# An attention kernel followed by two mixtures of experts: the first batch's pooled probabilities are turned ahead of its value sums, two of four token sums move to GpSimd, and the list of due times is set anew

## The chip, the cores and the metric

The kernel runs on one core of one Trainium2 chip. The metric is the device time of one execution in microseconds (us). The engines are named as in the profile: PE is TensorE's matrix multiply, PEld its weight load, DVE is VectorE, ACT is ScalarE, POOL is GpSimd, SP issues most of the transfers.

## The reference

Three stages follow each other; a sketch of what is computed:

```python
# q, k, v: [4 batches, 8 heads, 576 tokens, 64]
pooled = softmax(mean4(q) @ mean4(k).T / 8) @ mean4(v)   # 144 pooled tokens, each repeated 4 times
local  = softmax(where(|i - j| < 4, q @ k.T / 8, -1e9)) @ v
x = (repeat4(pooled) + local)           # -> [2304 tokens, 512]
h = x @ w_in                            # 512 -> 2048
x = (h * cos(h)) @ w_out                # 2048 -> 512
xn = x / sqrt(mean(x * x) + 1e-6) * rms_g
y = (silu(xn @ w_gate) * (xn @ w_val)) @ w_out2   # 512 -> 1536 -> 512
```

## The kernel before

**Tiles.** The 2304 tokens are nine tiles of 256. Attention makes them, batch by batch: `pooled` (L553) does one pair of heads of the pooled part, `block` one block of 116 tokens of the local part, `join` (L934) adds the two and `to_x` splits the sum into a high and a low part (L919 on ACT, L921 on POOL). The first product of experts runs in units of 512 columns, over a tile or a pair of tiles: `h` (L1200), then `kk` (L1218, ACT), `t` (L1220, DVE), the sine (L1223, ACT), the product with h (L1225, DVE), the high part `gh` (L1234, ACT), the low part `gl` (L1236, on DVE or POOL), and `y` (L1266), which multiplies `gh` and `gl` by the second weights. Tiles 0 to 4 go through alone (512 columns are then two weight slices of a 256-wide tile), tiles 5, 6 and 7, 8 in pairs. Each precise product is three fast ones (high by high, high by low, low by high). The gated product behind it (L1689, L1942) fills the second half of the time.

**The opening.** Before the first tile can start, SP loads the first heads of q and k, PE turns them (`qtr`, L680, in `turn`, L671), their tokens are summed in fours (L687, DVE), and `pooled` takes batch 0's four head pairs through scores (`sps`, L573), softmax (L578 to L594), a transpose of the probabilities (`tra`, L609), the value product (`avp`, L633) and a copy into `od`. The values' own pooled sums come from `pv` (L433). The local blocks run between: scores `bs` (L787 to L809), softmax (L825 to L830), transpose `bat` (L844), value product `bav` (L869), and L886 on DVE, which adds `od`. In the same stretch the weights of the first tiles are loaded and split on ACT, DVE (L319, L325) and POOL (L330).

**The order.** All of this is written as generators that yield (engine, planned time), wait for an event or take a buffer from a pool. The class `Order` plays them through with those planned times while the kernel is built: it starts the part that can start first, and takes the one with the earlier due time where two are near. Instructions are emitted in that order, so the order on each engine is fixed and is not decided on the chip. The constants on L32 to L57 are due times and planned costs of kinds of work: `PD`, `SD`, `VD` for steps of the pooled part, scores and value sums, `D1`, `DJ`, `BD`, `DU` for others, `LOADS` for the sequence in which SP issues raw tiles ("r"), weights ("w") and values ("v"), `SLACK` for how far parts may run ahead, `GLB` for the surcharge (us) at which `gl` is planned on DVE rather than POOL. Where a yield names two engines, the planned time with such a surcharge decides between them.

**Fillers.** `keep_warm` puts matrix products without a use (`warm<-ident`, L254) into gaps that the plan has on PE early on. Their number is the planned gap times `FR` over 0.22 us:

```python
n = int((t1 - max(t0, 2.5)) * (FR if t0 < FT else FR2) / 0.22)
```

Of the kernel before, what the change touches and what calls it, by code (L numbers as in the profile page):

```python
# [9 lines left out]
F32 = mybir.dt.float32  # L10
# [3 lines left out]
ALU = mybir.AluOpType  # L14
AX = mybir.AxisListType
# [16 lines left out]
EV = 400.0  # L32
W2X = 2
NRAW = 5
D1 = (-280, -320, 50)
DJ, BU = (-140, 8)
BD = (-300, -180)
NQK, NV = 2, 3
RAWT = 1.5
TRT = 0.46  # L40
SD, PD, VD = (-40, -200, -100)
LOADS = (("r", 3), ("w", 2), ("v", 5), ("w", 6),)
NCV = 5
FR = 1.1
FT = 90
FT2, FR2 = 215, 0.6
PB = 1
SLACK = 1.5
CU = 4
DS = 0  # L50
LG = 2
LK = int(LG < 8)
TP = 3
WD = 0.006
CVB, GLB = 9, 0.5
T0, T1, U1, U2 = 70, 52, 6.5, 4.26
DU = {"conv": 20, "pool": -180, "blk": -320}  # L57


class Order:  # L60
# [20 lines left out]
    def give(self, name, item, t=None):  # L81
        self.pools.setdefault(name, []).append((self.now() if t is None else t, item))
# [4 lines left out]
    @staticmethod  # L87
    def wait(ev):
        return "wait", ev

    @staticmethod
    def take(name, rest=0):
        return "take", name, rest
# [103 lines left out]
def fused_kernel(ctx: ExitStack, tc, q, k, v, w_in, w_out, w_gate, w_val, w_out2, rms_g, mask, bmask, out):  # L197
    nc = tc.nc
    PE, ACT, DVE, POOL, SP = nc.tensor, nc.scalar, nc.vector, nc.gpsimd, nc.sync
    S_ = Order()  # L200
    wait, take, give, done = S_.wait, S_.take, S_.give, S_.set
# [10 lines left out]
    ap = attn_ctx.enter_context(tc.tile_pool(name="ap", bufs=1, side="right"))  # L212
# [14 lines left out]
    def bank_tile(i, shape, name):  # L227
        return psum.tile(shape, F32, tag=f"b{i}", name=name)
# [13 lines left out]
    def keep_warm(t0, t1, p):  # L242

        own = p.pop("own", None)
        n = int((t1 - max(t0, 2.5)) * (FR if t0 < FT else FR2) / 0.22)
        have = [x for x in S_.pools["bank"] if x[0] <= t0]
# [8 lines left out]

    S_.fill = keep_warm if FR else None
    ysc = dram.tile([NTILE, 2, 128, DM], F32, name="ysc")
# [111 lines left out]
    PQ = {}  # L369
# [5 lines left out]
    od_t, od_i, ring = {}, {}, {}  # L375
# [138 lines left out]
    vd = {}  # L514
# [38 lines left out]
    def pooled(b, hp, E=None):  # L553
# [15 lines left out]
        x, y = PQ[b]  # L569
# [9 lines left out]
        for h2 in range(2):  # L579
            yield "ACT", 0.8, None, "exp"  # L580
            for q_ in range(2):
                o = E[:, q_, :, h2, :48]
                x = held[h2][1][:, q_].rearrange("p (c k) -> p c k", c=3)
# [7 lines left out]
        for q_ in range(2):  # L591
            _, e = yield [("POOL", 0.6), ("DVE", 0.36, None, None, 0.3)]
            x = E[:, q_, :, :, :48]
            (POOL if e == "POOL" else DVE).tensor_tensor(out=x, in0=x, in1=sm[:, q_].unsqueeze(1).unsqueeze(3).to_broadcast([72, 3, 2, 48]), op=ALU.mult)  # L594
        yield wait(("v", b, hp))
        vh, vi = vd[b, hp]
        if b not in od_t:
            od_i[b] = yield take("od")
            od_t[b] = ap.tile([128, 4, 144], F32, tag=f"od{od_i[b]}", name="od")
        a = "ax" if b == 0 and hp % 2 else "a"  # L600
        x = yield take(a)
        A = ap.tile([128, 3, 144], F32, tag=x, name="at") if a == "a" else x
# [10 lines left out]
        for c0, c1 in ((0, 2), (2, 3)):  # L613
            _, e = yield [("ACT", 0.05 + 0.13 * (c1 - c0), t0), ("DVE", 0.06 + 0.15 * (c1 - c0), t0, None, 0.3)]
# [5 lines left out]
        yield wait(("A", b, hp, 0))  # L620
        give("bank", i)
        give("att", "att")
        yield take("att")
        i = yield take("bank")
        o = bank_tile(i, [128, 144], "avp")
# [13 lines left out]
        _, e = yield [("ACT", 0.18), ("DVE", 0.22, None, None, 0.3)]  # L639
# [29 lines left out]
    QM, QL = {}, {}  # L669

    def turn(w, x, e, t):  # L671

        yield wait(("raw", w, x))
        yield take("att")
        i = yield take("bank")
        ps = bank_tile(i, [128, 2, 2, 128], "qtr")
        yield "PE", TRT
        for a in range(2):
            for r in range(2):
                PE.transpose(ps[:, a, r], t[:, 2 * a + e, 128 * r:128 * r + 128], ident)  # L680
        count(("rawf", w, x), 2)
        yield from turn_out(w, e, ps, QM[w, x], 512)
        give("bank", i)
        give("att", "att")
        if count2(("ts", w, x), 2):
            yield "DVE", 1.1
            DVE.tensor_reduce(out=PQ[0][w][:, 2 * x:2 * x + 2, 0:128], in_=QM[w, x].rearrange("p a (j r) -> p a j r", r=4), axis=AX.X, op=ALU.add)  # L687
            done(("ts", w, x))

    def turn_out(w, e, ps, part, n):  # L690
# [291 lines left out]
    def blk_due(b, u):  # L982
        if b == 0:
            return T0 + BD[0] if u < 3 else T0 + T1 + BD[1]
        if b == 1:
            return T0 + T1 * (S * b + 116 * u) / TT + D1[0]
        return T0 + T1 * S * b / TT + BU * u + DU["blk"]

    def blocks():

        yield wait("late")
        for b in range(1, B):
            for u in range(5):
# [7 lines left out]
                done(("raw", b, u))  # L1001
                S_.add(block(b, u, tuple(zip(t, r))), blk_due(b, u), slack=SLACK)

# [5 lines left out]
    def start():  # L1009
# [91 lines left out]
        first = {"r": 0, "v": 0}  # L1101
        for what, n in LOADS:
            if what == "w":
# [25 lines left out]
    def pool_ctl():  # L1129
# [3 lines left out]
        for b in range(1, B):  # L1133
            due = T0 + T1 * (9 * b / 4) + (D1[1] if b == 1 else DU["pool"])
            S_.due(due)
            if b == 1:
                S_.add(pq_part(b), due, slack=SLACK)
                yield wait(("pq", b))
                due += D1[2]
            for hp in range(4):  # L1140
                S_.add(pv(b, hp), due + 5.0 * hp)
                S_.add(pooled(b, hp), due + 5.0 * hp, slack=SLACK)
            yield wait(("pS", b))
# [891 lines left out]
```

## Time and profile before

| what | value |
|---|---|
| median of 3 runs | 968.74 us (967.98 to 969.39) |
| the profiled execution | 969.26 us, of which its span 967.5 us |
| PE busy | 943.6 us (98%) |
| DVE busy | 723.6 us (75%) |
| ACT busy | 552.2 us (57%) |
| POOL busy | 236.7 us (24%) |
| chain that ended last | PE 80%, DVE 7%, DMA 4%, issue 3% |

PE's busy time counts the fillers too. The profiled execution has 1.76 us outside its span, and is 0.52 us above the median. Times of the trace are counted from the span's start.

### The profile page before, as it was taken

How to read it: one execution, taken by the hardware profiler on the slowest of the kernel's cores; microseconds unless marked ns; L12 is line 12 of the kernel's file. 1: busy time of each engine (PE TensorE's matmuls, PEld its weight loads, DVE VectorE, ACT ScalarE, POOL GpSimd, SP SyncE). 2: the span in 40 equal slices, each digit the busy share in tenths (PEclk: the TensorE clock that was granted, in tenths of full speed). 3: DMA queues.
4: the chain of work that ended last, by engine and by line, in shares of the span. 5: the costliest groups of instructions: out<-in, count | busy, mean ns of one | idle time of the engine just before them, and what ended most of it. 6: DMA issues, size and time to landing. Idle time of an engine off the chain costs nothing.

```text
span 967.5 us, 18955 instructions
## 1 busy us (share of the span) xinstructions
PE 943.6 (98%) x7056; PEld 869.5 (90%) x7056; DVE 723.6 (75%) x1445; ACT 552.2 (57%) x1093; POOL 236.7 (24%) x273
## 2 busy tenths in 40 slices
PE   8899999999999998999999999999999999999998
PEld 8688788898898887788888889999999999999998
DVE  5989876677787656766485888586666678999885
ACT  5768886777787784774465664242232235454432
POOL 1576574421145423000050341000000015200000
PEclk9999999999999999999999999999999999999999
DMA  7668654566675536754323112143222243444432
GB/s 196 222 167 274 174 141 119 155 193 184 177 206 186 162 125 187 258 196 160 119 94 109 43 47 64 50 113 90 71 71 83 75 137 123 150 155 158 128 118 77
DMA packets 151404, 134.48 MB, mean 139 GB/s; under 512 B 61712, under 2 KB 127376, under 8 KB 151312
## 3 DMA queue, kind: packets, MB, share of 16 engines
q1 hardware_dynamic: 151312, 133.28, 45.2%
q8 instruction: 55, 0.90, 0.4%
q14 instruction: 37, 0.30, 0.1%
HBM read 93.53 MB, written 39.71 MB: 138 GB/s over the span
## 4 chain that ended last, share of the span: by engine, by line
PE 80%; DVE 7%; DMA 4%; issue 3%; ACT 2%; POOL 2%; SPq 1%; DVEq 0%; POOLq 0%; ACTq 0%
PE gvp L1689 26%; PE y L1266 17%; PE h L1200 16%; PE o L1942 14%; DMA rawwb<-in_moe_w_out 2%; PE bav L869 1%; PE btr L735 1%; DVE rawwa L325 1%; POOL wwa L330 1%; SPq L970 1%; DVE rawwa L319 1%; PE avp L629 1%; PE bs L793 1%; DMA y<-ysc 1%; PE yt L1594 1%
## 5 line engine op out<-in xcount | busy, mean ns | idle before, releaser
L1689 PE MATMUL gvp<-xc,wc 128*128 128x384 f32 x1296 | 231.7, 335 | 0.0
L1689 PEld LDWEIGHTS gvp<-xc,wc 128*128 128x128 f32 x1296 | 225.6, 188 | 0.3
L1760 DVE TENSOR_TENSOR tmp<-gvp,tmp 128x384 f32<-128x384 f32 x180 | 99.5, 554 | 54.8 <-PE gvp L1689 52.2
L1200 PE MATMUL h<-big,wwa 128*128 128x256 f32 (+1 forms) x756 | 123.8, 316 | 0.6 <-DVE t L1225 0.6
L1942 PE MATMUL o<-wo,wc 128*128 128x256 f32 x972 | 118.4, 280 | 0.0
L1200 PEld LDWEIGHTS h<-big,wwa 128*128 128x128 f32 x756 | 108.0, 190 | 10.4 <-DVE t L1225 0.9
L1942 PEld LDWEIGHTS o<-wo,wc 128*128 128x128 f32 x972 | 115.7, 190 | 0.0
L1266 PE MATMUL y<-wwa,big 128*128 128x512 f32 x432 | 108.8, 397 | 0.5 <-DVE big L1236 0.5
L1266 PEld LDWEIGHTS y<-wwa,big 128*128 128x128 f32 x432 | 79.0, 188 | 16.9 <-DVE big L1236 1.1
L1200 PE MATMUL h<-big,wwb 128*128 128x256 f32 (+1 forms) x504 | 83.3, 317 | 0.0
L1266 PE MATMUL y<-wwb,big 128*128 128x512 f32 x324 | 80.5, 395 | 0.5 <-DVE big L1236 0.5
L1200 PEld LDWEIGHTS h<-big,wwb 128*128 128x128 f32 x504 | 71.8, 190 | 6.8 <-issue 0.8
L1220 DVE SCALAR_TENSOR_TENSOR t<-kk,h 128x512 f32<-128x512 int32 x72 | 48.9, 680 | 38.1 <-ACT kk L1218 36.3
L1266 PEld LDWEIGHTS y<-wwb,big 128*128 128x128 f32 x324 | 59.5, 188 | 13.2 <-DVE big L1236 0.8
L1218 ACT ACTIVATE kk<-h 128x512 int32<-128x512 f32 x72 | 42.7, 593 | 45.2 <-PE h L1200 44.3
L1225 DVE TENSOR_TENSOR t<-h,t 128x512 f32<-128x512 f32 x72 | 49.3, 686 | 23.5 <-ACT t L1223 23.4
L1223 ACT ACTIVATE t<-t,cst 128x512 f32<-128x512 f32 x72 | 51.9, 723 | 19.5 <-DVE t L1220 19.0
L1751 ACT ACTIVATE tmp<-gvp 128x384 f32<-128x384 f32 x36 | 17.7, 492 | 76.1 <-PE gvp L1689 76.1
L1826 POOL TENSOR_TENSOR wt<-wo 128x256 f32<-128x256 f32 x10 | 9.7, 973 | 209.1 <-DVE wc L1545 183.5
L1885 ACT ACTIVATE wc<-ut 128x512 fp32r<-128x512 f32 (+1 forms) x60 | 34.3, 584 | 42.5 <-DVE ut L1871 25.2
L1234 ACT ACTIVATE big<-t 128x512 fp32r<-128x512 f32 x72 | 44.9, 627 | 20.3 <-DVE t L1225 19.9
L1236 DVE TENSOR_TENSOR big<-t,big 128x512 fp32r<-128x512 f32 x57 | 43.9, 771 | 12.9 <-ACT big L1234 12.3
(212 smaller groups left out, 1693.0 us busy)
## 6 DMA issues: line engine op xcount, KB each, us to landing
us<-tmp SPq DMA_DIRECT2D x72, 192.0 KB, 2.0
uf<-us SPq DMA_DIRECT2D x48, 256.0 KB, 2.9
rawwa<-in_moe_w_out SPq DMA_DIRECT2D x21, 512.0 KB, 5.0
wfs<-rawwa SPq DMA_DIRECT2D x36, 256.0 KB, 2.5
rawwa<-in_moe_w_gate SPq DMA_DIRECT2D x12, 512.0 KB, 4.0
rawwa<-in_moe_w_val SPq DMA_DIRECT2D x12, 512.0 KB, 4.3
wf<-wfs SPq DMA_DIRECT2D x12, 512.0 KB, 3.9
vb<-in_v SPq DMA_DIRECT2D x80, 64.0 KB, 2.6
```

The lines of the kernel that those rows point to most:

```text
L1200: PE.matmul(h[:, w_ * ci:w_ * ci + w_], a[:, ksl], x_at(x, kk), start=m == 0, stop=m == 11)
L1218: ACT.activation(out=kk, in_=h, func=ACTF.Copy, scale=INV2PI, bias=0.25)
L1220: DVE.scalar_tensor_tensor(out=t, in0=kk, scalar=TWOPI, in1=h, op0=ALU.mult, op1=ALU.subtract)
L1223: ACT.activation(out=t, in_=t, func=ACTF.Sin, scale=-1.0, bias=cst[:, 0:1])
L1225: DVE.tensor_tensor(out=t, in0=h, in1=t, op=ALU.mult)
L1234: ACT.activation(out=gh, in_=t, func=ACTF.Copy)
L1236: (POOL if e == "POOL" else DVE).tensor_tensor(out=gl, in0=t, in1=gh, op=ALU.subtract)
L1266: PE.matmul(y[j][b], g[:, tsl], a, start=(first and ci == 0 and i == 0), stop=(last and c == 15 and i == 2))
L1689: PE.matmul(bank, w[:, a, kk], xc[:, x, b, kk], start=first and i == 0, stop=i == 5, skip_group_check=True)
L1760: DVE.tensor_tensor(out=half(o), in0=a, in1=half(b), op=ALU.add)
L1885: ACT.activation(out=o[:, 0], in_=src, func=ACTF.Copy)
L1942: PE.matmul(b[m][1][:, l], u[0][x][:, j, l], w[:, y, k], start=(p == 0 and l == 0 and i == 0), stop=(p == C3 - 1 and i == 2), skip_group_c ...
```

## The change

In `pooled`, for batch 0 alone, the wait for the value sums and the taking of `od` move from ahead of the transposes to behind them and behind the copies of their result. In `turn`, each token sum may be planned on POOL, as three additions, instead of one reduction on DVE. The rest are constants.

```diff
-D1 = (-280, -320, 50)
-DJ, BU = (-140, 8)
-BD = (-300, -180)
+D1 = (-280, -380, 50)
+DJ, BU = (-200, 8)
+BD = (-200, -180)
+TB = -1.2
-SD, PD, VD = (-40, -200, -100)
-LOADS = (("r", 3), ("w", 2), ("v", 5), ("w", 6),)
+SD, PD, VD = (-40, -20, -400)
+LOADS = (("r", 3), ("w", 4), ("v", 2), ("w", 2), ("v", 3), ("w", 4),)
-FR = 1.1
+FR = 1.4
-SLACK = 1.5
+SLACK = 2
-CVB, GLB = 9, 0.5
+CVB, GLB = 9, 0.7
-DU = {"conv": 20, "pool": -180, "blk": -320}
+DU = {"conv": 20, "pool": -240, "blk": -280}
...
-        yield wait(("v", b, hp))
-        vh, vi = vd[b, hp]
-        if b not in od_t:
-            od_i[b] = yield take("od")
-            od_t[b] = ap.tile([128, 4, 144], F32, tag=f"od{od_i[b]}", name="od")
+        if b:
+            yield wait(("v", b, hp))
         a = "ax" if b == 0 and hp % 2 else "a"
...
         give("att", "att")
+        if not b:
+            yield wait(("v", b, hp))
+        vh, vi = vd[b, hp]
+        if b not in od_t:
+            od_i[b] = yield take("od")
+            od_t[b] = ap.tile([128, 4, 144], F32, tag=f"od{od_i[b]}", name="od")
         yield take("att")
...
         if count2(("ts", w, x), 2):
-            yield "DVE", 1.1
-            DVE.tensor_reduce(out=PQ[0][w][:, 2 * x:2 * x + 2, 0:128], in_=QM[w, x].rearrange("p a (j r) -> p a j r", r=4), axis=AX.X, op=ALU.add)
+            _, g = yield [("DVE", 1.1), ("POOL", 2.2, None, None, TB)]
+            o, y = PQ[0][w][:, 2 * x:2 * x + 2, 0:128], QM[w, x].rearrange("p a (j r) -> p a j r", r=4)
+            if g == "DVE":
+                DVE.tensor_reduce(out=o, in_=y, axis=AX.X, op=ALU.add)
+            else:
+                POOL.tensor_tensor(out=o, in0=y[:, :, :, 0], in1=y[:, :, :, 1], op=ALU.add)
+                for r in (2, 3):
+                    POOL.tensor_tensor(out=o, in0=o, in1=y[:, :, :, r], op=ALU.add)
```

Since the plan is played through anew, instructions move on every engine. The line numbers of the changed kernel are one higher than before up to L596 and two lower at the transposes (L607); from L684 on they are 4 to 10 higher (`gl` L1246, `y` L1276).

**PE, where batch 0's probabilities are first turned** (`tra`). Before, ahead of the first transposes (L609) stand the local scores of more head pairs, the sums of values `pv` and the transposes of the local part (`bat`); of the stretch between the first `pv` and the first `avp` the part that counts is this:

```order
L433 MATMUL pv<-vb,sel 128x256 x2
L809 MATMUL bs<-bst,ident 128x256
L254 MATMUL warm<-ident 128x128 x2
L609 MATMUL tra<-ident,E 128x72 x6
L844 MATMUL bat<-ident,bE 128x128 x4
L609 MATMUL tra<-ident,E_115 128x72 x6
L633 MATMUL avp<-at,vs 64x144 x6
```

In the changed kernel the same place on PE reads:

```order
L574 MATMUL sps<-pqs 72x144 x4
L819 MATMUL bs<-bst,ident 128x256 x2
L434 MATMUL pv<-vb,sel 128x256 x2
L607 MATMUL tra<-ident,E 128x72 x6
L434 MATMUL pv<-vb,sel 128x256 x3
L607 MATMUL tra<-ident,E_115 128x72 x6
L854 MATMUL bat<-ident,bE 128x128 x4
```

The first two transposes now stand among the first five `pv`, ahead of every `bat`, and the value products `avp` follow much later.

**PE, from the last value product of batch 0 to the first `h`.** Before:

```order
L633 MATMUL avp<-at,vs 64x144 x6
L633 MATMUL avp<-E_114,vs 64x144 x6
L809 MATMUL bs<-bst,ident 128x256
L869 MATMUL bav<-bt,vb 64x58 x48
L809 MATMUL bs<-bst,ident 128x256
L254 MATMUL warm<-ident 128x128 x12
L844 MATMUL bat<-ident,bE 128x128 x4
L254 MATMUL warm<-ident 128x128 x5
L1200 MATMUL h<-big,wwa_300 128x256 x12
```

In the changed kernel:

```order
L607 MATMUL tra<-ident,E_117 128x72 x6
L255 MATMUL warm<-ident 128x128 x2
L637 MATMUL avp<-at,vs 64x144 x6
L637 MATMUL avp<-E_114,vs 64x144 x6
L255 MATMUL warm<-ident 128x128 x4
L879 MATMUL bav<-bt,vb 64x58 x48
L255 MATMUL warm<-ident 128x128 x10
L854 MATMUL bat<-ident,bE 128x128 x4
L255 MATMUL warm<-ident 128x128 x9
L879 MATMUL bav<-bt,vb 64x58 x16
L854 MATMUL bat<-ident,E_114 128x128 x4
L1210 MATMUL h<-big,wwa_322 128x256 x12
```

25 fillers instead of 17 stand between the last `tra` and `h`, a further `bav` and `bat` come ahead of `h`, and two `bs` are gone from there. In all the changed kernel has 92 fillers, before 70; the first run, at the program's start, has 33 instead of 26.

**PE, where single tiles give way to pairs** (the 12 last columns of `h` for a tile alone are 128x256, the first of a pair 128x512). Before:

```order
L1200 MATMUL h_4802<-big_93,wwa9_1972 128x256 x12
L1200 MATMUL h_4802<-big_93 128x256 x12
L1266 MATMUL y_4535<-wwa12_1613,big_93 128x512 x3
L1266 MATMUL y_4536<-wwa12_1613,big_93 128x512 x3
L1266 MATMUL y_4535<-wwa14_1860,big_93 128x512 x3
L1266 MATMUL y_4536<-wwa14_1860,big_93 128x512 x3
L1266 MATMUL y_4535<-big_93 128x512 x3
L1266 MATMUL y_4536<-big_93 128x512 x3
```

In the changed kernel (of the y the rows of one output bank, 4579; the other, 4580, has as many):

```order
L1210 MATMUL h_4873<-big_93 128x256 x12
...
L1276 MATMUL y_4579<-wwa17_1482,big_93 128x512 x3
...
L1276 MATMUL y_4579<-wwa18_1642,big_93 128x512 x3
...
L1276 MATMUL y_4579<-wwa14_1751,big_93 128x512 x3
...
L1210 MATMUL h_4955<-big_93,wwa0_322 128x512 x12
L1276 MATMUL y_4579<-big_93 128x512 x3
L1276 MATMUL y_4580<-big_93 128x512 x3
```

Before, 12 products `y` stand between the last `h` of a single tile and the `y` that uses its result (the rows without a weight's name). In the changed kernel 24 of `y` and 12 wide ones of `h` stand there.

**POOL and DVE.** Of the 72 subtractions `gl`, 57 stood on DVE and 15 on POOL; now it is 17 and 55. Two of the four token sums of `turn` are on POOL, as six additions.

## Rows read from the trace of the kernel before

**Rows 1.** Windows, PE alone: stretch, length, busy (passes), granted clock, DMA share, GB/s.

```profile
0.00:70.75 70.75, 62.57 (x759) 1.00 0.69 192
70.75:132.00 61.25, 57.59 (x541) 1.00 0.72 210
132.00:190.00 58.00, 55.32 (x475) 1.00 0.49 135
372.00:383.00 11.00, 7.79 (x27) 0.84 0.58 188
383.00:968.00 585.00, 578.34 (x3487) 1.00 0.35 113
```

**Rows 2.** Windows, the fillers (L254) alone: PE busy, PEld busy.

```profile
0.00:70.75 70.75, 18.39 (x124) 17.39 (x124) 1.00 0.69 192
70.75:132.00 61.25, 1.32 (x8) 1.05 (x8) 1.00 0.72 210
132.00:190.00 58.00, 1.16 (x8) 0.97 (x8) 1.00 0.49 135
```

**Rows 3.** Timeline, PE, opening: start, length, line, form, passes, [idle before, releaser].

```profile
1.36 8.68 PE L254 MATMUL warm<-ident 128*128 128x128 f32 x52 [1.36 <-POOL ident masks.py:199]
...
19.97 1.20 PE L573 MATMUL sps<-pqs 64*72 64x144 f32 x16
...
38.09 1.03 PE L433 MATMUL pv<-vb,sel 128*128 128x256 f32 x4
...
45.80 0.97 PE L609 MATMUL tra<-ident,E 72*128 72x72 f32 x12
...
53.83 2.84 PE L254 MATMUL warm<-ident 128*128 128x128 f32 x24
...
57.98 1.68 PE L1200 MATMUL h<-big,wwa 128*128 128x256 f32 x12
```

**Rows 4.** Windows, all engines: length, then PE, PEld, DVE, ACT, POOL busy.

```profile
20.76:46.63 25.87, 21.08 (x265) 16.57 (x261) 24.46 (x55) 18.30 (x60) 13.03 (x10) 1.00 0.70 220
70.75:132.00 61.25, 57.59 (x541) 49.94 (x540) 56.92 (x87) 50.95 (x93) 41.02 (x44) 1.00 0.72 210
```

**Rows 5.** Timeline, DVE and POOL: a token sum, and an addition of 128x256.

```profile
12.62 1.22 DVE L687 TENSOR_REDUCE pqs<-qm 128x256 f32<-128x1024 f32 x1
...
57.69 0.73 POOL L382 TENSOR_TENSOR pq<-pq 128x256 f32<-128x256 f32 x1
```

**Rows 6.** Timeline, SP's queue: the issues of the first values.

```profile
8.75 17.29 SPq L970 DMA_DIRECT2D vb<-in_v  x20
```

**Rows 7.** Timeline, DVE and POOL: a weight step alone, beside POOL, and POOL's.

```profile
36.49 0.68 DVE L325 SCALAR_TENSOR_TENSOR rawwb<-rawwb 128x512 int32<-128x512 int32 x1
...
42.59 1.45 DVE L325 SCALAR_TENSOR_TENSOR rawwb<-rawwb 128x512 int32<-128x512 int32 x1
...
37.95 5.54 POOL L330 TENSOR_TENSOR wwa<-rawwb,wwa 128x512 fp32r<-128x512 f32 x3 [2.04 <-ACT wwa L327]
```

**Rows 8.** Timeline, PE and POOL, from batch 1's last value product to tile 2.

```profile
175.67 0.90 PE L629 MATMUL avp<-at,vh 128*128 128x144 f32 x6
...
189.81 2.40 PE L1200 MATMUL h<-big,wwa 128*128 128x256 f32 x18
...
183.89 1.99 POOL L921 TENSOR_TENSOR big<-bt,big 128x464 fp32r<-128x464 f32 x2
```

**Rows 9.** Timeline, PE and DVE, where single tiles give way to pairs.

```profile
372.18 2.91 PE L1266 MATMUL y<-wwa,big 128*128 128x512 f32 x12
...
378.80 4.38 PE L1266 MATMUL y<-big 128*128 128x512 f32 x11 [2.34 <-DVE big L1236]
...
377.54 1.21 DVE L1236 TENSOR_TENSOR big<-t,big 128x512 fp32r<-128x512 f32 x1
```

**Rows 10.** Groups of the subtraction `gl`: count, busy, mean ns, then idle time before.

```profile
L1236 DVE TENSOR_TENSOR big<-t,big 128x512 fp32r<-128x512 f32 x57 | 43.9, 771 | 12.9 <-ACT big L1234 12.3
...
L1236 POOL TENSOR_TENSOR big<-t,big 128x512 fp32r<-128x512 f32 x15 | 20.7, 1383 | 80.4 <-ACT big L1234 67.2 <-PE h L1200 8.8 <-issue 4.4
```

## The prediction

> **What bounds the kernel now.** The page's busy shares come first: PE is at work for 943.6 of 967.5 us, and the chain that ended last is PE for four fifths. The products that count are the same in both kernels (every line on PE has the same count but the fillers), so the time can change only by PE's idle time, by its fillers, and by time at the lower clock. I therefore cut the span into stretches and took for each its length minus PE's busy time plus its fillers. From 0 to 70.75 us, where the first `y` starts, 70.75 − 62.57 + 18.39 = 26.6 us are lost; to 132 it is 61.25 − 57.59 + 1.32 = 5.0, to 190 it is 58.00 − 55.32 + 1.16 = 3.8 [rows 1, 2]. Then PE is full up to 372. From 372 to 383 it is idle for 11.00 − 7.79 = 3.2 us, and its granted clock is 0.84 of the stretch, which at 11 us is another 11 × 0.16 = 1.8: 5.0 us lost [rows 1]. Behind 383 it idles for 6.7 us in 585, and nothing that the change moves stands there. So the change can gain or lose in four places, and I go through these. I count the sum against the profiled execution (969.26 us, 0.52 above the median of the runs) and take 0.52 off at the end.
>
> **The opening, up to the first `h`.** The limit here is not PE but DVE: between the first softmax and the end of batch 0's last transposes it is busy for 24.46 of 25.87 us, in 55 instructions, 0.445 us each [rows 4]. What the change takes from DVE ahead of that stretch is two token sums of 1.22 us [rows 5], but they lie between loads there and not on the path. On POOL each becomes three additions. No row before has this form; the nearest is an addition of 128x256 at 0.73 us, so 2.2 us for a sum, and with operands four apart up to twice that. Both ends are over before the 20 us at which the scores start [rows 3], so I cost them at nothing; with that cover gone they would cost 1 to 3 us.
>
> The structural edit lets the transposes of the first head pairs go ahead of their value sums. What it frees is PE's wait for them, and PE was not the limit. The first ones move forward, but the transposes of the last pair, on which the last `avp` and then `bav`, the sum L886 and `to_x` hang, move back: in the order of DVE, 64 instructions instead of 55 now stand up to the last head pair's transposes (more conversions of weights, the softmax of the local blocks). At 0.445 us that is +4.0 us: 46.8 becomes some 50.7. From there to the first `h` it took 57.98 − 46.77 = 11.2 us [rows 3]. Two steps of local scores drop out of that piece, a part of a `bav` and one `bat` enter it, which I count together as −0.5, an estimate by their passes; eight more fillers enter too, and 12 of them took 2.84 us, so 8 × 0.237 = +1.9. The piece comes to 12.6, and the first `h` to 63.2 us (+5.2). The first `y` I put 12.6 us behind that, at 75.8 instead of 70.75. One more `h` run of about 1.5 us (1.68 with the overlap at its end) stands ahead of it, which is work brought forward, so the loss is **+3.6 us**. The bounds are +0 (DVE's nine more instructions fit in its 1.4 us of idle and under the fillers) and +6 (the nine are conversions of 0.7 us each, 6.3, and nothing gives way).
>
> The first run of fillers goes from 26 to 33: at 0.118 us a pass (2.84 / 24) that is 14 × 0.118 = 1.7 us more on PE ahead of the first transposes of q and k, and at the 0.167 of this first run (8.68 / 52) 2.3. The scores at 19.97 wait for the last loads and not for PE, so it costs nothing; if it did, those 1.7 to 2.3 would be the price. The values are loaded with weights ahead of and among them: 20 issues took 17.29 us, 0.86 each with the waits between [rows 6], so four issues ahead of the values' end cost 3.5 us, from 26.0 to 29.5. They are first used by `pv` at 38.09 [rows 3]: hidden by 8.6 us, unless `pv` moves to below 30.
>
> **From the first `y` to 132.** DVE stays the limit, with 56.92 of 61.25 us busy [rows 4], so a late start can be caught up only in its 4.3 us of idle time, and in what its own load shrinks. Five of the subtractions of this stretch go to POOL, and the conversions done early are gone from here; by my count of the rows that remain DVE has some 1.1 us less to do between its first and ninth L1220. The lateness of 3.6 us is thus caught up by something between 0 and 3.6. I take 2.7, three quarters, since both give 5.4 us of room but half of DVE's idle pieces lie ahead of work that PE must deliver. The two stretches together: **+0.9**, bounds −3 and +6.
>
> **From 132 to 190.** The fillers fall from four to two, at 1.16 / 4 each: −0.6. PE's waits for `gl` on DVE fall a little as the load falls: −0.5, bounds 0 and −1.6 (all of the 3.8 us lost there, less fillers and a second 1 us). Against that, tile 2 needs batch 1's last `avp`, its copy, the transfer of the local part, the sum and POOL's split. Before, `avp` started at 175.67 and `h` of the tile at 189.81: 14.1 us with work between, in which POOL's split was done at 185.88 [rows 8], 9.3 us behind the end of `avp`. Now the order leaves only 12 + 12 of `y`, 12 of `h` and three small transposes there, 2.9 + 1.6 + 2.9 + 0.7 = 8.1 us. 9.3 − 8.1 = 1.2 us of wait: **+0.1** together, bounds −1.6 and +2.5.
>
> **Where single tiles give way to pairs, 372 to 383.** Before, the last unit of tile 4 is on its way through ACT and DVE while PE has 2.91 us of `y` to do, and then waits, 2.34 us of it for `gl` on DVE at 377.54, whose end is 378.75 [rows 9]. Behind that wait the clock falls to its lower level. Now 24 of `y` and 12 of `h`, all 512 wide, lie between the last narrow `h` and its `y`: three times 2.9 are 8.7 us, against the 6.6 from 372.18 to the end of `gl`. The wait goes, and with it the fall of the clock: −5.0. What stays: `gl` is now on POOL for most units, and POOL took 1.38 us for one where DVE took 0.77 [rows 10], so the `y` one unit ahead sees its result 0.6 later; and the first tile of the next pair is joined late. I leave 1.1 us for both: **−3.9**, bounds −5.0 and −1.
>
> **The sum.** +0.9 + 0.1 − 3.9 = −2.9: 969.26 − 2.9 = 966.4 for a profiled execution, 965.8 on the median (− 0.52).
>
> **A rule that speaks against the change.** In the saturated stretch L325 takes 0.68 us on DVE when POOL is idle, and 1.45 beside POOL's L330, whose three take 1.85 each [rows 7]: 0.77 us lost per 1.85 of POOL, 0.42 us for each. The Trainium skill, page "SBUF — State Buffer", section "Who interferes with whom", says that a DVE instruction with two SBUF inputs and a GpSimd instruction that reads SBUF share one port pair, and that whoever comes second waits for the whole of the other; the rows agree with a lock in part, as the price is less than POOL's whole 1.85. By it the work handed to POOL is not free for DVE but comes back as waits; the trace decides the size, which is taken below.
>
> **The rivals.** (D) *POOL holds DVE up, slower.* To 132 us POOL gets some 11 us more (six additions of 0.73, five subtractions of 1.38). At 0.42 that is 4.6 us of DVE, at half of it (where only some of DVE's instructions have two inputs in SBUF) 2.3; I take 3.5. In a stretch where DVE is the limit this uses up what room there was, the 3.6 of the opening stay, and the sum is 3.6 + 3.5 + 0.1 − 3.9 = +3.3: 972.0. It decides from the point where DVE's idle time to 132 falls to zero. For it speaks that DVE is at 93 to 95% in both windows; against it, that most of the moved subtractions lie behind 190, where PE is full and DVE has room. (B) *The opening is not caught up, but POOL does no harm.* 3.6 + 0.1 − 3.9 = −0.2: 968.5, no change. (C) *The opening is caught up wholly.* PE's early transposes let the first local blocks join sooner, DVE's order has no cost, −2.3 there, −1.2 behind it, and −5.0 at the pairs: −8.5, 960.2. For it speaks that 26.6 us are lost in the opening, the most of any stretch; against it, DVE's count. (E) *The change does nothing net* in any place: 968.7.
>
> **How the numbers follow.** The forecast (A) has 0.40, B 0.22, D 0.18, C 0.15, E 0.05. A measurement of this kernel tells changes of about 0.2% (1.9 us) from none. A reaches from 963.5 to 967.5, so some 0.36 of it is faster by more than that; with C that is 0.51. B, E and the rest of A make 0.28, D and B's upper edge 0.21. The range leaves out the outer half of C and the upper half of D: 961.5 to 971. The forecast's own range is 963.5 to 967.5.
>
> **What would show it.** In the changed trace the first `h` should stand near 63 and the first `y` near 75.8 us; if they stand at or below 58 and 71, the count on DVE was the wrong measure of the opening, and C holds. Two L325 in the saturated stretch at 1.4 us where one stood before, and DVE without idle time to 132, would show D. The wait of 2.34 us and the fall of the clock near 380 should be gone, and it is the surest step. A wait of about 1.2 us ahead of tile 2's first `h`, near 190, should be new. The forecast is wrong most easily in the opening, whose three quarters are an estimate.

## The result, and the profile after

The changed kernel takes 975.59 us (median of 6 runs, 973.68 to 978.93), the kernel before on the same chip 969.84: a ratio of 1.006, interval 1.0042 to 1.0077, slower by some 5.8 us where 2.9 faster was forecast. A repetition gave 1.0067 (1.0043 to 1.0091). One execution of the kernel before, of 4583 us at a granted clock of 0.19, is left out of all figures. The profiled execution has a span of 973.3 us, 5.8 above the one before.

The page of the changed kernel, busy time and share of the span:

```profile
span 973.3 us, 19079 instructions
PE 950.3 (98%) x7100; PEld 874.4 (90%) x7100; DVE 709.9 (73%) x1430; ACT 540.2 (55%) x1072; POOL 294.6 (30%) x309
```

DVE has 13.7 us less to do, POOL 57.9 more, PE 6.7 more, nearly all of it fillers. The windows of PE in the changed kernel, as in [rows 1], cut at its first `y` (76.80) and from 190 us on at the same times as before; 76.80 to 190 is cut in two 61.2 us behind the first `y`, where before it was 61.25, and of 383 to the end the two parts up to 600 are shown:

```profile
0.00:76.80 76.80, 71.60 (x812) 0.98 0.66 186
76.80:138.00 61.20, 57.87 (x545) 1.00 0.72 208
138.00:190.00 52.00, 51.59 (x490) 1.00 0.50 135
190.00:372.00 182.00, 177.38 (x1708) 1.00 0.61 181
372.00:383.00 11.00, 10.78 (x62) 1.00 0.67 219
383.00:490.00 107.00, 106.70 (x489) 1.00 0.53 178
490.00:600.00 110.00, 104.77 (x506) 1.00 0.17 60
```

The fillers alone (PE busy, PEld busy), as in [rows 2]:

```profile
0.00:76.80 76.80, 24.46 (x166) 22.80 (x166) 0.98 0.66 186
76.80:190.00 113.20, 2.76 (x18) 2.33 (x18) 1.00 0.62 175
```

And of the kernel before the windows that the prediction did not look at one by one:

```profile
190.00:372.00 182.00, 182.00 (x1778) 1.00 0.60 177
383.00:490.00 107.00, 105.65 (x485) 1.00 0.54 182
490.00:600.00 110.00, 108.97 (x538) 1.00 0.19 67
```

Length minus PE busy plus fillers, and the clock's share where it is below 1, is the loss of a stretch. Set beside the prediction's terms:

| stretch | loss before | loss after | difference | forecast |
|---|---|---|---|---|
| to the first `y` | 26.6 | 5.2 + 24.5 + 1.4 (clock) = 31.1 | +4.5 | +3.6 |
| first `y` to 190 | 8.8 | 3.7 + 2.8 = 6.5 | −2.3 | −2.6 |
| 190 to 372 | 0 | 4.6 | +4.6 | 0 |
| 372 to 383 | 5.0 | 0.2 | −4.8 | −3.9 |
| 383 to 490 | 1.4 | 0.3 | −1.1 | 0 |
| 490 to 600 | 1.0 | 5.2 | +4.2 | 0 |

The sum is +5.1 of the 5.8 by which the spans differ. The first, second and fourth lines came out close to the forecast (the second only as a sum, see below); the two places where nothing was expected cost 8.8 us.

These are PE's waits there, by its timeline (in brackets the idle time and what ended it):

```profile
192.94 4.46 PE L1210 MATMUL h<-big,wwa 128*128 128x256 f32 x35 [0.97 <-POOL big L931]
212.67 3.14 PE L1210 MATMUL h<-big,wwb 128*128 128x256 f32 x24 [0.31 <-ACT bt L861]
269.72 0.66 PE L854 MATMUL bat<-ident,bt 128*128 128x128 f32 x4 [1.47 <-DVE bt L755]
298.15 1.44 PE L1276 MATMUL y<-wwa,big 128*128 128x512 f32 x5 [1.71 <-DVE big L1246]
...
509.71 1.38 PE L1604 MATMUL yt<-ident,y 128*128 128x128 f32 x8 [2.50 <-DVE y L1624]
522.56 0.72 PE L1604 MATMUL yt<-ident,y 128*128 128x128 f32 x4 [0.57 <-ACT y L1622]
568.00 2.81 PE L1276 MATMUL y<-big 128*128 128x512 f32 x11 [1.02 <-DVE big L1246]
```

Most end with DVE. What DVE does ahead of the longest, and POOL beside it (timelines of both engines):

```profile
504.62 0.66 DVE L1584 TENSOR_SCALAR nst<-nst 128x2 int32<-128x2 int32 x1
505.32 1.21 DVE L1586 SCALAR_TENSOR_TENSOR nst<-nst 128x2 f32<-128x2 f32 x1
506.56 1.20 DVE L1587 TENSOR_TENSOR nst<-nst 128x2 f32<-128x2 f32 x1
507.80 0.16 DVE L1588 SCALAR_TENSOR_TENSOR nst<-nst 128x2 f32<-128x2 f32 x1
...
504.52 0.73 POOL L1539 TENSOR_TENSOR wt<-wf,wt 128x256 f32<-128x256 f32 x1
505.22 2.53 POOL L1555 TENSOR_TENSOR wc<-wt,wc 128x512 fp32r<-128x512 f32 x2
```

A step on two numbers for each partition takes 0.16 us, and 1.2 as long as each of POOL's two subtractions (1.27 us) runs beside it. The chain of these small steps feeds `yt` on PE. In the kernel before these steps meet POOL as well (four of its instructions of 0.74 us; 0.72, 0.59 and twice 0.66 us between 502.99 and 505.92), and PE does not wait there.

### The profile page after: what moved, and what is told of

Its sections match the earlier page's. It is cut to its first block, busy times and chain, and to the rows that moved or that the text cites. A ratio compares the mean times of both kernels' runs of the same rounds, so it can differ in the third digit from the quotient of the medians.

```text
span 973.3 us, 19079 instructions
## 1 busy us (share of the span) xinstructions
PE 950.3 (98%) x7100; PEld 874.4 (90%) x7100; DVE 709.9 (73%) x1430; ACT 540.2 (55%) x1072; POOL 294.6 (30%) x309
## 4 chain that ended last, share of the span: by engine, by line
PE 78%; DVE 11%; DMA 4%; ACT 3%; issue 2%; POOL 0%; SPq 0%; DVEq 0%; ACTq 0%; POOLq 0%
PE gvp L1699 26%; PE h L1210 16%; PE y L1276 14%; PE o L1952 13%; PE warm L255 2%; PE bav L879 2%; DMA rawwa<-in_moe_w_out 1%; DMA y<-ysc 1%; PE btr L745 1%; DMA bt<-loc 1%; DVE xc L1678 1%; PE bs L803 1%; PE avp L633 1%; PE bat L854 1%; DVE nst L1586 1%
## 5 line engine op out<-in xcount | busy, mean ns | idle before, releaser
L1246 POOL TENSOR_TENSOR big<-t,big 128x512 fp32r<-128x512 f32 x55 | 73.8, 1342 | 174.5 <-ACT big L1244 134.3
L1276 PE MATMUL y<-wwa,big 128*128 128x512 f32 x432 | 109.2, 397 | 1.7 <-DVE big L1246 1.7
L1276 PEld LDWEIGHTS y<-wwa,big 128*128 128x128 f32 x432 | 78.7, 188 | 18.1 <-DVE big L1246 2.0
L1276 PE MATMUL y<-wwb,big 128*128 128x512 f32 x324 | 81.6, 396 | 0.2 <-POOL big L1246 0.2
L1276 PEld LDWEIGHTS y<-wwb,big 128*128 128x128 f32 x324 | 59.3, 188 | 12.6 <-POOL big L1246 0.5
```

The source lines that it names most:

```text
L1246: (POOL if e == "POOL" else DVE).tensor_tensor(out=gl, in0=t, in1=gh, op=ALU.subtract)
L1276: PE.matmul(y[j][b], g[:, tsl], a, start=(first and ci == 0 and i == 0), stop=(last and c == 15 and i == 2))
```

## The experiments

All were timed beside the kernel before, whose median stands in the fourth column (us):

| run | what | median | before | ratio (interval) |
|---|---|---|---|---|
| x1 | changed, gl's engines as before | 972.83 | 968.83 | 1.0045 (1.0027 to 1.0063) |
| x2 | before, gl's engines as changed | 974.49 | 968.83 | 1.0050 (1.0033 to 1.0066) |
| x3 | changed, FR 1.1 | 973.95 | 968.83 | 1.0056 (1.0037 to 1.0075) |
| x4 | before, GLB 0.7, new order | 972.76 | 968.83 | 1.0036 (1.0018 to 1.0054) |
| x5 | changed, again | 975.93 | 969.19 | 1.0067 (1.0043 to 1.0091) |
| x6 | changed, gl and FR as before | 970.49 | 969.19 | 1.0016 (0.9999 to 1.0034) |
| x7 | before, edit in `pooled` alone | 974.35 | 969.19 | 1.0044 (1.0023 to 1.0065) |
| x8 | changed, all token sums on DVE | 978.89 | 969.19 | 1.0094 (1.0067 to 1.0121) |
| x9 | as x6, FR 0.7 | 970.96 | 969.98 | 1.0013 (0.9995 to 1.0032) |
| x10 | as x6, the later gl as changed | 973.11 | 969.98 | 1.0040 (1.0022 to 1.0058) |
| x11 | before, two token sums on POOL | 968.47 | 969.98 | 0.9989 (0.9970 to 1.0008) |
| x12 | before, FR 0.7 | 969.95 | 969.98 | 1.0002 (0.9986 to 1.0019) |
| x13 | changed, two L1555 on DVE | 973.57 (one run) | 969.50 | |
| x14 | as x11, all gl on DVE | 966.36 | 969.50 | 0.9969 (0.9955 to 0.9984) |

One thing makes most of these clean: the engine that an instruction is given, and the number of fillers, can be changed where it is emitted, behind the planner's back, so that the order on the other engines stays as it was. Three theories were set against each other. **Theory 1**: the subtractions moved to POOL are the cost. **Theory 2**: the new order is. **Theory 3**: the fillers are.

### Engines of gl, and fillers, one at a time

x1, in the changed kernel (x2 does the same in the kernel before with the 55 numbers of the changed one):

```diff
         _, e = yield [("POOL", 1.5), ("DVE", 0.8, None, None, GLB)]
+        e = "POOL" if n in {4, 14, 15, 19, 20, 25, 28, 29, 32, 35, 43, 44, 58, 63, 70} else "DVE"
```

> The changed kernel with its order on every engine kept; only the 72 subtractions gl are put on the engines that they had before (57 DVE, 15 POOL). Theory 1 (the subtractions on POOL hold DVE up and come late): PE's waits that are new from 190 to 370 us and from 490 to 600 us, 4.5 and 4.2 us, go for the most part, 967 to 970 us. Theory 2 (the new order itself makes these waits): 974 to 977 us, within 1.5 us of the changed kernel, the waits at the same places. Theory 3 (the fillers): no change either, 975.

> The kernel before with its order kept; only the engines of the 72 subtractions gl are those of the changed kernel (17 DVE, 55 POOL). Theory 1: slower by 4 to 8 us, 974 to 978. Theory 2 and 3: 968 to 971; the wait of 2.34 us at 378 and the lower clock behind it stay, since the order that makes them stays.

x3, in the changed kernel:

```diff
-FR = 1.4
+FR = 1.1
```

> The changed kernel with FR back at 1.1: 72 fillers instead of 92, all else in the same order. Theory 3: the first h comes 4 us earlier and the time falls by 3 to 5 us, 971 to 973. Theories 1 and 2: DVE sets the opening and the first h comes at most 2 us earlier, and by 180 us no more than 1 is left: 974 to 976.

x4, in the kernel before, the order played through anew:

```diff
-CVB, GLB = 9, 0.5
+CVB, GLB = 9, 0.7
```

> The kernel before with GLB at 0.7 alone, the order played through anew: 16 gl on DVE and 56 on POOL, 73 fillers. Theory 1: the new waits of 190 to 370 and 490 to 600 us come with it and outweigh the gain where tiles give way to pairs: 970 to 975. Theory 2: gain at the pairs of 4 to 5 us alone, 964 to 967. Theory 3: the same, 964 to 967.

No theory came through whole. x2 came out within theory 1's numbers, +4.9 us, and x4 too, although 12 wide `h` stand ahead of the last `y` of the single tiles in its order as in the changed kernel (its profiled execution ran at a granted clock of 0.944 throughout, so only its times and its order are used). But x2's trace does not bear theory 1 out. PE idles for 0.6 us from 190 to 372 and 0.6 from 490 to 600, against 0 and 1.0 in the kernel before, and it is already 3.0 us late at the first `y` (73.72), ahead of which POOL has no gl in either. Most of what it lost there is a meeting of DVE and POOL on other work:

```profile
39.87 3.68 DVE L827 TENSOR_SCALAR bst<-bst 128x8 f32<-128x8 f32 x1
...
39.73 3.79 POOL L330 TENSOR_TENSOR wwa<-rawwb,wwa 128x512 fp32r<-128x512 f32 x3
```

The same step took 0.56 us in the kernel before. Whether the executions of x2 without a trace had this meeting too is not known, so its 4.9 us can't be put down to gl. But x1 gave back only 1.5 to 2.2 of the changed kernel's 6, and fell outside what either theory had said; its waits at 193, 213 and 297 us are still there (0.99, 0.31 and 1.72 us), so those are not gl's. x3 gave back 0.4 to 1.1, less than theory 3 wanted, though its first `h` stood at 61.53 instead of 64.44.

### Both together, the edit alone, the token sums

x5 is the changed kernel again; x6 takes the edits of x1 and x3 together; x7 is the kernel before with the two pieces of `pooled` from the diff and nothing else; x8 is this, in the changed kernel:

```diff
             _, g = yield [("DVE", 1.1), ("POOL", 2.2, None, None, TB)]
+            g = "DVE"
```

> The changed kernel once more, beside the three that follow, for a second trace and a time on the same chip. Expected 974 to 976 us, 0.5 to 0.7% above the kernel before. If the waits of 1.71 us at 298 (y for gl on DVE) and of 2.50 us at 509 (yt for DVE) are there again, they belong to the order; if they move or go, they are a meeting of DVE and POOL that differs from one execution to the next.

> The changed kernel in its own order, with the engines of gl and the number of fillers as before. If GpSimd's subtractions and the fillers are the cost (theories 1 and 3 together): 968 to 970 us, the loss gone. If the order that the due times make costs more than both (theory 2): 972 to 974, and the waits at 193 and 298 us are still there.

> The kernel before with only the edit in pooled (batch 0's wait for the value sums behind the transposes), played through anew; 63 fillers, 59 gl on DVE. My reckoning of the opening (DVE sets it, the edit frees only PE): 968 to 971, and the first h within 2 us of before, 57.98. Rival: the earlier transposes free the opening, the first h is at 55 or below and the time 964 to 967.

> The changed kernel in its own order, with all four token sums on DVE (the two that were planned on POOL stay at their place in the order). If the sums on POOL cost nothing, as I reckoned: 974 to 977 us, as the changed kernel in the same call, within 1.5 us. If they hold the scores up or hold DVE up: 1 to 3 us faster. If they helped: 1 to 3 us slower, with the first scores sps behind 21 us.

x5 has the waits at 298 and 510 again (1.92 and 2.50): they belong to the changed kernel and not to one execution. x6 lands between the two expectations: engines of gl and fillers together make it 1.0016 instead of 1.0060 and 1.0067, some 4.3 to 4.9 us of the loss, and what is left of the order is +1.6 us, which its interval hardly tells from none.

x7 went the wrong way for both of its expectations: the edit alone costs 4.3 us. Its PE shows where: the last transposes of batch 0 end at 51.0 instead of 46.8 and the first `h` is at 63.38, and the wait at the pairs is longer than before [rows 9]:

```profile
382.82 0.66 PE L1203 MATMUL h<-big,wwa 128*128 128x512 f32 x1 [4.94 <-ACT big L922]
384.51 5.06 PE L1203 MATMUL h<-big,wwa 128*128 128x512 f32 x11 [1.03 <-POOL big L924]
```

A good part of the late opening is the meeting that x2 has: at 40.45 DVE's step of 128x8 (L830 here) takes 3.68 us beside POOL's three splits. It starts 0.45 us later than before, and the product behind it that `bat` waits for ends at 45.08 instead of 42.33: 2.3 of the 4.2 us come from this meeting. So x7 doesn't show what the edit costs without this meeting.

x8 hints that the token sums on POOL are a gain in this order: without them 2.6 us are lost against x5, of which the two intervals (2.3 and 2.6 us to either side) leave little certain. Its scores start at 20.49, not behind 21, and 9.22 us behind the first transposes of q and k (`qtr`), where it is 8.56 us in the changed kernel, x1 and x5: some 0.7 us are shown. The rest was not traced to one place.

### Fillers further down, which gl, and the token sums in the order of before

x9 is x6 with FR at 0.7. x10 is x6 with the condition of x1 only for `n < 40`, the units of single tiles. x12 sets FR to 0.7 in the kernel before. x11, in the kernel before, sums the second and third tile as the changed kernel does:

```diff
+    DVE_SUMS = ((0, 0), (1, 1))
...
-            DVE.tensor_reduce(out=PQ[0][w][:, 2 * x:2 * x + 2, 0:128], in_=QM[w, x].rearrange("p a (j r) -> p a j r", r=4), axis=AX.X, op=ALU.add)
+            o, y = PQ[0][w][:, 2 * x:2 * x + 2, 0:128], QM[w, x].rearrange("p a (j r) -> p a j r", r=4)
+            if (w, x) in DVE_SUMS:
+                DVE.tensor_reduce(out=o, in_=y, axis=AX.X, op=ALU.add)
+            else:
+                POOL.tensor_tensor(out=o, in0=y[:, :, :, 0], in1=y[:, :, :, 1], op=ALU.add)
+                for r in (2, 3):
+                    POOL.tensor_tensor(out=o, in0=o, in1=y[:, :, :, r], op=ALU.add)
```

> The changed kernel in its own order, gl on the engines of before and FR at 0.7: 41 fillers (before 70, the changed kernel 92). If each filler in the opening is lost time, the first h comes another 3 to 4 us earlier than with 72 (60.3 us) and the time falls to 966 to 968. If PE's clock falls for want of work, or DVE sets the opening by then, nothing is won: 969 to 972, with a granted clock under 1 in the opening.

> The changed kernel in its own order with 72 fillers; gl on the engines of before only in the 40 units of the single tiles, beside attention (34 on DVE and 38 on POOL in all). If GpSimd's subtractions cost where attention keeps DVE busy: 970 to 971, as with all of gl as before. If they cost in the pairs' part, behind 370 us: 973 to 974, as with fewer fillers alone.

> The kernel before in its own order; two of the four token sums are done by GpSimd at their place, as in the changed kernel. If DVE's token sums were on the way to the first scores: sps starts at 18 to 18.7 instead of 19.97, and the time is 966 to 968. If they were beside it, as the prediction said: no change, 968 to 970.

> The kernel before with FR at 0.7: 44 fillers instead of 70, all else in the same order. If fillers stood in the way here too: 965 to 967, first h near 55. If DVE sets the opening here: no change, 968 to 970. If the clock falls for it: slower, 971 or more, with a granted clock under 1 before 70 us.

The start of the first scores and the first `h` follow the fillers in both orders. PE's timeline in x6, x9 and x12, in this order:

```profile
16.89 1.21 PE L574 MATMUL sps<-pqs 64*72 64x144 f32 x16
...
60.33 1.68 PE L1210 MATMUL h<-big,wwa 128*128 128x256 f32 x12
```

```profile
16.14 1.21 PE L574 MATMUL sps<-pqs 64*72 64x144 f32 x16
...
59.26 1.67 PE L1210 MATMUL h<-big,wwa 128*128 128x256 f32 x12
```

```profile
17.42 1.20 PE L573 MATMUL sps<-pqs 64*72 64x144 f32 x16 [0.28 <-DVE pqs L720]
...
55.08 0.36 PE L1200 MATMUL h<-big,wwa 128*128 128x256 f32 x1
56.39 1.57 PE L1200 MATMUL h<-big,wwa 128*128 128x256 f32 x11 [0.94 <-POOL big L921]
```

So fillers did stand in the way of the scores, 2.5 us of it in the kernel before [rows 3] and 1.9 to 3.2 in the changed one. These sizes are rough, since the first run of 52 passes alone took from 7.59 (x6) to 9.01 us (x2). But the time of x12 does not move, and that of x9 not against x6. What is won goes to the granted clock. PE's windows up to 190 us in x6, x9 and x12, in this order (before, the clock is 1.00 there [rows 1]):

```profile
0.00:190.00 190.00, 178.09 (x1813) 0.99 0.65 183
```

```profile
0.00:190.00 190.00, 176.67 (x1745) 0.95 0.64 180
```

```profile
0.00:190.00 190.00, 172.80 (x1719) 0.98 0.63 181
```

Idle time and fillers together fall from 33.7 to 28.2 us between x6 and x9, and from 35.4 to 32.0 between the kernel before and x12, and the clock takes some 7.6 (0.04 of 190) and 3.8 us back. This is not one execution: over all runs the mean granted clock is 0.9962 in x6 and 0.9915 in x9, 0.9954 in the kernel before and 0.9923 in x12, which of 970 us are 4.6 and 3.0. x9 came out as its second expectation said. x12 has the time that was expected of DVE, with the lower clock that was expected of the third.

x10 bears on the place of gl's cost. It differs from x6 only in the 32 units of the pairs, and is at 1.0040 against 1.0016: 2.3 us, about as much as the two intervals together leave open. Its `yt` waits 2.52 us at 509 and `y` 0.98 at 568, as in the changed kernel; in x6 the first is 1.46 and the second is not there. Against x3, from which it differs in the single tiles' units, it gains 1.5 us by the ratios, within what these can't tell from nothing.

PE's idle time of all traces in the changed order says it more firmly. From 490 to 600 us it is 4.7 to 5.3 us where the pairs have gl on POOL (the changed kernel, x3, x5, x8, x10, x13), 3.7 to 3.8 where they have it as before (x1, x6, x9), and 1.0 in the kernel before: some 1.3 us are gl's, 2.7 the order's. From 190 to 372 us it is 3.5 to 5.5 us with the single tiles' gl as changed, and 2.7 to 5.1 with it as before (x1, x6, x9, x10): gl makes no difference there that can be told.

How gl costs its 1.0 us ahead of the longest wait stands on DVE, a few us earlier. The changed kernel (DVE, then POOL), and then DVE in x6:

```profile
496.11 2.39 DVE L1678 TENSOR_TENSOR xc<-xs,xc 128x512 fp32r<-128x512 f32 x2
498.42 1.23 DVE L1678 TENSOR_TENSOR xc<-yn,xc 128x512 fp32r<-128x512 f32 x1
...
496.65 1.29 POOL L1246 TENSOR_TENSOR big<-t,big 128x512 fp32r<-128x512 f32 x1 [0.80 <-ACT big L1244]
497.97 1.13 POOL L1678 TENSOR_TENSOR xc<-yn,xc 128x256 fp32r<-128x256 f32 x1
```

```profile
491.23 1.28 DVE L1679 TENSOR_TENSOR xc<-xs,xc 128x512 fp32r<-128x512 f32 x2
...
493.03 0.68 DVE L1679 TENSOR_TENSOR xc<-yn,xc 128x512 fp32r<-128x512 f32 x1
```

Beside POOL's gl, and the POOL step that follows it, three of DVE's instructions take 3.6 us instead of 2.0; the gl that DVE no longer does there took 0.68 in x6. The small steps ahead of `yt` take 1.2 us twice in x1 and x6 as well, so their meeting with POOL's split is the order's and not gl's.

x11 starts the scores at 19.08 instead of 19.97 [rows 3], short of the 18 to 18.7 that was expected, and 0.43 us of that is a shorter first run of fillers (8.25 and 8.68); the first `h` stands at 57.05. Its time, 1.1 us less, has an interval that includes no change.

### What holds DVE up

x13, in the changed kernel, takes POOL's two subtractions of 512 away from DVE's small steps; x14 takes POOL's last 15 subtractions gl away in x11:

```diff
         _, e = yield lo_on(m, c < EARLY)
+        if m == 512:
+            e = "DVE"
```

```diff
         _, e = yield [("POOL", 1.5), ("DVE", 0.8, None, None, GLB)]
+        e = "DVE"
```

> The changed kernel with only the two subtractions of 128x512 (L1555, 2.53 us on GpSimd at 505 us) on DVE, at their place. If DVE's steps on 128x2 take 1.2 us each because GpSimd's subtraction runs beside them, they take 0.16 to 0.7 there now and the wait of 2.50 us ahead of yt falls by 1 us or more, though DVE has two instructions of 0.69 us more. If DVE is merely behind with its own work, the steps take 1.2 us still, or the wait grows.

> The kernel before in its own order, two token sums on GpSimd, all 72 gl on DVE (15 were on GpSimd). If GpSimd's subtractions cost more than DVE's wherever they stand, it beats the kernel before by more than the sums alone: 965 to 967. If DVE has no room for them beside attention: 969 to 972, with new waits of y for gl on DVE before 190 us.

DVE's and PE's timeline of x13, at the place of the rows of 504 us above:

```profile
503.35 0.66 DVE L1586 TENSOR_SCALAR nst<-nst 128x2 int32<-128x2 int32 x1
504.04 0.16 DVE L1588 SCALAR_TENSOR_TENSOR nst<-nst 128x2 f32<-128x2 f32 x1
504.24 0.16 DVE L1589 TENSOR_TENSOR nst<-nst 128x2 f32<-128x2 f32 x1
...
505.69 0.69 DVE L1557 TENSOR_TENSOR wc<-wt,wc 128x512 fp32r<-128x512 f32 x1
```

```profile
506.82 1.38 PE L1606 MATMUL yt<-ident,y 128*128 128x128 f32 x8 [0.89 <-DVE y L1626]
```

The two steps of 1.2 us take 0.16, and PE's wait falls from 2.50 to 0.89, although DVE has one more instruction of 0.69 on the way and another behind. That is theory 1's mechanism at this place, with POOL's own weight split as the one that holds, and not gl. It is worth next to nothing, though: the waits behind it grow, and from 490 to 600 us PE idles for 5.0 us against 5.2 in the changed kernel:

```profile
520.82 0.73 PE L1606 MATMUL yt<-ident,y 128*128 128x128 f32 x4 [1.72 <-ACT y L1624]
566.65 2.81 PE L1276 MATMUL y<-big 128*128 128x512 f32 x11 [1.36 <-DVE big L1246]
```

x14 is faster than both kernels, as its first expectation said: 0.9969, interval 0.9955 to 0.9984, 3 us below the kernel before. Its trace has no new wait of `y` for gl, so DVE had the room. Its one trace doesn't show where the 3 us come from (its span, 967.6, is not below the one before, with a dip of the clock near 105 us). The mean granted clock of its runs is 0.9970, of the kernel before beside it 0.9952, which is 1.7 us of 967; why it is higher, and which of the 15 count for the rest, stays open.

## Why the prediction was wrong

**The opening: right in kind.** DVE's count was 64 instructions up to the last transposes and an end at 50.7; measured are 63, busy for 29.2 us, and an end at 52.0. First `h` at 63.2 forecast, 64.44 measured; first `y` 75.8 and 76.80. The loss was put at +3.6, and is +4.5. But one sentence in it failed: "The scores at 19.97 wait for the last loads and not for PE, so it costs nothing". The first transposes of q and k, on which the scores hang, come behind the first run of fillers, and that took 10.32 us instead of 8.68; with FR back at 1.1 the scores start at 18.14 (x3) and 16.89 (x6). I had counted eight fillers on the way to `h` and let the first run's go free; the price that was named for them, 1.7 to 2.3 us, was the one to take. Likewise the token sums were not off the path, as I had them ("between loads there and not on the path"): with two of them on POOL the way from the first `qtr` to the scores is 9.63 us in x11 instead of 10.10, and 8.56 in the changed kernel against 9.22 in x8.

**To 190: the sum right, by luck.** It is −2.3 against −2.6, but I had 2.7 us caught up ahead of the place that is 132 before, and +0.1 behind it. The loss of the first part went up, from 5.0 to 3.3 of idle time and 2.8 of fillers, 6.1; that of the second fell from 3.8 to 0.4. DVE, which "stays the limit" in my account, is busy for 51.92 of the first part's 61.20 us, where it was 56.92 of 61.25, and three gl of that part stand on POOL instead of one, two more and not five. The new wait ahead of tile 2 was forecast at 1.2 us near 190, and a wait of 0.97 for POOL's split stands at 192.94.

**The pairs: right.** 24 of `y` and 12 of `h` cover the way of gl, the wait of 2.34 is 0.22, and the clock stays at 1.00 where it was 0.84: −4.8 against −3.9.

```profile
376.19 1.43 PE L1276 MATMUL y<-wwb,big 128*128 128x512 f32 x5 [0.22 <-POOL big L1246]
```

**The step that failed** is the first one, on what bounds the kernel: "Then PE is full up to 372", and behind 383 "nothing that the change moves stands there". Both were read from the kernel before and carried over to the changed one. That PE is full in the old order says that each wait there is just covered, not by how much. Due times and the subtractions' engines change up to the end of the first product, near 570 us, and 4.6 and 4.2 us of waits came up there. With gl's engines and the number of fillers as before (x6) 2.7 and 2.6 us of these are left, so most of the 8.8 us is the new order's; of the rest some 1.3 us, from 490 to 600, are gl's on POOL in the pairs' units.

**Rival D had the mechanism in part, and the wrong place.** It said that POOL holds DVE up, 972.0, chance 0.18, and put all its cost ahead of 132 us; against it I wrote that "most of the moved subtractions lie behind 190, where PE is full and DVE has room". In the changed order it is the later ones whose cost can be seen; for those beside attention none can be told from nothing. The point from which it decides was wrong as well: it does not need DVE's idle time at zero. From 430 to 600 us in the changed kernel DVE is busy 115 of 170 us, and PE waits for it all the same, because what stands ahead of `yt` in DVE's queue is stretched beside POOL's instructions. Its 972.0 is the slowest of the rivals, and still 3.6 us short.

**The sum by parts.** From x1, x3, x6 and the two runs of the changed kernel (+4.5, +5.6, +1.6, +6.0 and +6.7 thousandths), each part taken twice and averaged: gl on POOL 4.0 (x3 to x6) and 1.8 (changed to x1), so about 2.9; fillers 2.9 (x1 to x6) and 0.7 (changed to x3), about 1.8; the rest of the order 1.6. Each has an interval of about two thousandths, so what is shown is that gl and the fillers together make most of the net loss, not the share of each. The traces give the fillers more: idle time and fillers up to 190 us are 35.4 to 36.3 us with 92 of them (changed, x1, x5, x13) and 32.3 to 33.7 with 72 (x3, x6, x10), some 3 us. And the order's 1.6 is small because two larger terms meet in it: 5.3 us of waits behind 190 in x6, against some 6 that it wins from 372 to 490, where tiles give way to pairs.

The Trainium skill's rule, page "SBUF — State Buffer", section "Who interferes with whom", was weighed as a price on DVE's total time. That the shared port pair is "an exclusive lock" is what the rows above show for steps with two inputs in SBUF: at 505 us 0.16 us becomes 1.21, and the step ends with POOL's instruction of 1.27. Blocks that outlast one instruction are in the last section.

## What to carry to other kernels

A wait of zero in the old order is no measure of its slack: where a change replays the whole plan, look in each stretch for the shortest cover between producer and consumer, and count what the change does to that. An instruction given to GpSimd has two prices, its own longer time and what it adds to DVE's instructions beside it; the second counts where TensorE waits for what stands behind these in DVE's queue, however idle DVE is on average. But read it from a whole stretch: in x13 a wait fell by 1.6 us, and the next two grew by 1.5. Fillers in gaps of a plan are free only if the plan's gap is there on the chip, and leaving them out may cost clock: try their count by itself, and set the time that is won beside the granted clock of all runs. And where a change moves the time of a few unrelated instructions, look in its trace ahead of the first place that it touches: x2 lost 3 us there.

## What the runs showed of the hardware that was not expected

The block can last over two or three of POOL's instructions: three in x2 and x7 near 40 us, with 3.68 us for a step of 128x8 that takes 0.16 alone, and there POOL was held up first, for 4.18 us on a product of 72x288 (L594) that takes 0.67. Again in x2, DVE's weight step starts just ahead of a pair of POOL's and ends behind both: 3.13 us where it takes 0.68 alone [rows 7], and PE waits 2.17 us for what is queued behind it (timelines of DVE, POOL and PE in x2):

```profile
129.14 3.13 DVE L325 SCALAR_TENSOR_TENSOR rawwa<-rawwa 128x512 int32<-128x512 int32 x1 [1.27 <-ACT rawwa L323]
...
129.18 2.54 POOL L330 TENSOR_TENSOR wwa<-rawwa,wwa 128x512 fp32r<-128x512 f32 x2
...
132.88 0.71 PE L254 MATMUL h<-ident 128*128 128x128 f32 x4 [2.17 <-DVE bt L883]
```

In the kernel before, the same pair of steps did not meet so, and PE waited 0.62 us there.

The granted clock of 30 to 50 us differs between kernels and executions: 1.00 in the kernel before, x6, x11 and x14, 0.91 in the changed kernel, x2, x3, x12 and x13, 0.83 in x1, x5, x7, x8, x9 and x10. PE's idle time there does not tell them apart (4.2 us in the kernel before, 1.8 in x9), nor does the number of fillers (92 in x5, 41 in x9, both 0.83), though over all runs the clock is lower with fewer of them (x9 and x12 above). At 0.83 of 20 us some 3 us are lost, as much as the parts that were sought; the runs of the kernel before lie between 965.6 and 974.0 us, and this may be one reason.

A step with a single input is held up too: L1584, on two numbers for each partition, took 0.66 us beside POOL's subtraction of 0.73 in the changed kernel and in x13, and the same step without POOL beside it 0.17.
